# One constant in a hand-written order: the fourth Fourier sum of each batch at step 47 instead of step 48

## The chip, the cores and the metric

The kernel runs on one core of a Trainium2 chip, in float32. The metric is the device time of one execution in microseconds (us). Before the change three runs gave 2300.13, 2300.18 and 2295.85 us, so the median is 2300.13 us.

A core has five instruction streams that run side by side and wait for each other by semaphores: TensorE (PE in the profile, its weight loads PEld), VectorE (DVE), ScalarE (ACT), GpSimd (POOL) and SyncE (SP), which here only issues DMAs. Each stream runs its own instructions in the order in which they were put.

## The reference

Two blocks follow one another, for 8 batches, 12 heads, 448 positions and head width 64:

```python
scores = scale * np.matmul(q, k.transpose(0, 1, 3, 2))
scores = np.einsum('bhij,hg->bgij', scores, w_pre)
attn = softmax(scores)
attn = np.einsum('bhij,hg->bgij', attn, w_post)
x = np.matmul(attn, v)                 # then (B,H,S,D) -> (B,S,H*D)
mixed = real(fft(fft(x, axis=1), axis=2))
u = x + mixed
out = u + relu(layernorm(u) @ w_ch1) @ w_ch2
```

The first block is attention whose heads are mixed by a 12x12 matrix before and after the softmax. The second adds a two-dimensional Fourier transform of the attention's output to it, and then a feed-forward layer of width 3072.

## The kernel before, in words

**Two phases.** `mix_phase` computes u for all batches and writes it to DRAM in two tensors per batch, `u_scr` and `u_rev`. `ffn_phase` does the feed-forward layer and fills the rest of the time. In the profile the mixing phase ends at about 797 us.

**Steps.** The mixing phase is one loop over steps `s`. A batch has 23 steps, so batch b starts at step f = 23b. Each step s carries, for different rows, a softmax pipeline: "pre" (L656, mixes heads on PE from the gathered scores `Kr` into PSUM tiles `mx`), "max" (L663, DVE), "exp" (L670, ACT, into `PP`), "scale" (reciprocal on DVE at L677 and L678, then two multiplications on POOL at L680), "post" (L690, mixes heads again on PE into the PSUM tile `po`) and "turn" (L703, DVE, transposes `po` into `Pv`). "pre", "max", "exp" and "scale" of step s work for step s+2, "post" and "turn" for step s itself. "gather" (L645) issues four DMAs on SP that reorder the copied scores `Sb` into `Kr` for step s+5; `Sb` has two buffers, each for a block of three steps (one block has two), and a buffer is free when the gathers of its block have landed.

**What is put between.** Four lists hold further work with the step at which it is due. "QK" is a run of scores (L628 on PE, two PSUM tiles, copied to `Sb` by ACT at L489). "AV" is attention times v (L720, two PSUM tiles, copied to `XT` by ACT). "full" holds the transposes of q and k (L601), the turn of a finished group of rows into a tile `X` (L764, copied by ACT), `emit_z` (the first Fourier transform, L829), and `emit_s2`, the second: eight matmuls at L845 into one PSUM tile, after which DVE adds the result into two `X` tiles by four instructions (L856 and L858). A batch has four of these sums, two pairs of rows by two parities; their steps are `AT_S`. After the second parity of a pair a store goes to a list `later`, and in the "scale" part of the first step that begins with the store in that list, it is issued: an indirect DMA to `u_rev` by POOL (L868) and a DMA `u<-X` to `u_scr` on SP (L877). For pair 1 a further single row goes out on POOL (L874) two steps after that. "none" holds loads; those of v (`vv`, L581) are issued by POOL at steps 48 to 52 counted from the batch two before. `folds` are sums and differences of `X` tiles on POOL (L785, L790, L799) that `emit_z` reads later; two are issued per step after the scaling.

**PSUM.** Scores, attention times v, transposes and Fourier sums share one ring of four PSUM tiles named `ms`. A run of scores or of attention times v takes two of them, a Fourier sum one. PE waits when the tile whose turn it is has not been copied out or added yet. The copies of what is pending are put by `flush`.

**The order in a step.** On PE, DVE, ACT and POOL the order of the program is kept. It differs between even and odd steps:

```python
ORDERS = ("pre post flush AV max0 exp0 QK max1 exp1 turn scale conv full gather",
          "pre post flush max0 max1 QK exp0 AV turn exp1 scale conv gather full flush")
```

(The strings are joined here; the first is for even steps.) "conv" is one DVE operation of the preparation of the feed-forward weights (L250 to L310). On SP the order is chosen by the scheduler, which plans with its own estimates. In even steps what "full" leaves pending is flushed after the next step's "post".

**Around the change.** Steps are counted here from the start f of the batch whose sums are meant, so "step 47" is f+47. At step 46 there are a run of scores, the third Fourier sum and a turn into `X`; at step 47 a run of scores and one of attention times v; at step 48 two runs of scores and the fourth Fourier sum; at step 49 and at step 50 one run of each again; at steps 51 and 52 a run of scores and a turn into `X`. For even batches step 47 is odd and step 48 even; for odd batches the other way round. Batch 7 is not concerned, since its sums are done in the feed-forward phase in the order of the list. In batch 6 steps 47 and 48 lie behind the last softmax step, and step 47 also holds `lead.turn`, a transposition for the feed-forward phase.

Of the kernel before, what the change touches and what calls it, by code (L numbers as in the profile page):

```python
# [95 lines left out]
AT_AV = ((1, 2, 4), (0, 1, 3), (1, 3, 5), (1, 3, 4))  # L96
AT_X = ((13, 0), (23, 1), (28, 3), (29, 2))
AT_Z = (39, 40, 40, 42)
AT_S = ((42, 44), (46, 48))

ORDERS = tuple(o.split() for o in (
    "pre post flush AV max0 exp0 "
# [348 lines left out]
def mix_phase(ctx, tc, rest, ident, q, k, v, w_pre, w_post, u_scr, u_rev, wts, lead):  # L451
# [433 lines left out]
    def due(kind, at, fn):  # L885
        fill[kind].append((at, len(fill[kind]), fn))
# [4 lines left out]
    for b in range(B):  # L891
# [41 lines left out]
        for pair in range(2):  # L933
            for par in range(2):
                due("full", f + AT_S[pair][par],
                    lambda b=b, pair=pair, par=par: emit_s2(b, pair, par))
# [617 lines left out]
```

## Time and profile before

| what | value |
| --- | --- |
| median of three runs | 2300.13 us (2295.85 to 2300.18) |
| the profiled execution's own time | 2299.42 us |
| its span, first to last instruction | 2297.6 us |
| mean granted TensorE clock | 0.998 |
| busy: PE, PEld, DVE, ACT, POOL | 98%, 76%, 74%, 51%, 56% of the span |
| matmuls of the Fourier sums at L845 | 256, median 326 ns |
| adds of the Fourier sums at L856 and L858 | 64 and 64, 0.55 us each |

How to read it: the busy share of PE counts modelled ends of pipelined matmuls, so the length of a step is read from the starts of its instructions in the timeline. The list of waits says in total what an engine waited for, how often, and the longest single wait. In a timeline, brackets name the idle time ahead of an instruction and what ended it. The chain of work goes back from the last instruction of a window to what released it. In slices of 57.4 us the mixing phase takes about the first 14 of 40.

### The profile page before, as it was taken

The numbers are of one execution on the slowest core, as the hardware profiler recorded it, in microseconds if no ns is written. First come the engines' busy times: TensorE is split into PE (matmuls) and PEld (weight loads), VectorE is DVE, ScalarE is ACT, GpSimd is POOL, SyncE is SP. The second block draws the span as 40 slices with busy tenths as digits, with TensorE's granted clock in tenths as the row PEclk, the third lists the DMA queues.
The fourth block names the chain that finished last, engine by engine and source line by source line (L and its number), as shares of the span: only waits on it lengthen the run. The fifth ranks groups of instructions, "written<-read, shape, count | busy, mean of one in ns | idle before, by whom it ended". The sixth has DMA issues, their size and how long they took to land.

```text
span 2297.6 us, 60793 instructions
## 1 busy us (share of the span) xinstructions
PE 2249.2 (98%) x22894; PEld 1740.7 (76%) x22894; DVE 1711.2 (74%) x3640; ACT 1167.1 (51%) x3330; POOL 1292.1 (56%) x1805
## 2 busy tenths in 40 slices
PE   7999999999999999999999999999999999999998
PEld 3455555555554677777899999999999899999998
DVE  5778787888877757776877787778778777765545
ACT  4676767767676533231445445444444445434434
POOL 7677878879768541221555555546555645454334
PEclk9999999999999999999999999999999999999999
DMA  7566565666756475649677887788787987795664
GB/s 185 168 178 181 168 192 171 190 179 181 202 151 190 143 265 182 230 162 327 191 181 180 252 214 184 212 195 242 204 197 184 277 188 174 191 257 121 143 146 76
DMA packets 228063, 439.45 MB, mean 191 GB/s; under 512 B 35964, under 2 KB 149558, under 8 KB 227772
## 3 DMA queue, kind: packets, MB, share of 16 engines
q1 hardware_dynamic: 156620, 301.52, 38.2%
q0 software_dynamic: 68864, 133.00, 30.4%
q8 instruction: 183, 3.00, 0.6%
q10 hardware_dynamic: 2288, 1.05, 0.2%
q14 instruction: 108, 0.88, 0.1%
HBM read 213.16 MB, written 143.16 MB: 155 GB/s over the span
## 4 chain that ended last, share of the span: by engine, by line
PE 87%; DVE 5%; DMA 3%; ACT 2%; issue 1%; POOL 1%; SPq 1%; ACTq 0%; DVEq 0%; POOLq 0%
PE psP L1213 18%; PE psP L1335 14%; PE psR L1213 9%; PE psR L1335 7%; PE mx L656 6%; PE ms L720 6%; PE ms L628 5%; PE po L690 5%; PE psQ L1213 4%; PE psQ L1335 3%; PE psP L1290 3%; PE ms L845 2%; PE ms L601 2%; DMA Kr<-Sb 1%; PE psR L1290 1%
## 5 line engine op out<-in xcount | busy, mean ns | idle before, releaser
L1369 POOL DMA_DIRECT2D out_dram<-od x172 | 209.1, 1276 | 261.7 <-DVE od L1357 175.3
L680 POOL TENSOR_SCALAR PP<-PP,rcp 128x448 f32<-128x448 f32 x368 | 234.6, 647 | 170.2 <-DVE rcp L678 123.8
L670 ACT ACTIVATE PP<-mx,nmx 128x448 f32<-128x448 f32 x368 | 230.2, 631 | 165.2 <-DVE nmx L663 157.2
L663 DVE TENSOR_REDUCE nmx<-mx 128x1 f32<-128x448 f32 x368 | 212.5, 618 | 101.2 <-PE mx L656 99.1
L1176 POOL TENSOR_TENSOR hq<-h 128x128 f32<-128x128 f32 (+1 forms) x210 | 130.0, 619 | 255.9 <-ACT h L1235 122.3
L1363 ACT COPY od<-psP 128x192 f32<-128x192 f32 x488 | 156.1, 320 | 172.0 <-PE psP L1335 170.6
L1366 DVE TENSOR_TENSOR od<-od 128x768 f32<-128x768 f32 x210 | 201.3, 972 | 52.7 <-ACT od L1363 52.3
L703 DVE STREAM_TRANSPOSE Pv<-po 128x896 f32<-128x896 f32 x184 | 203.7, 1107 | 2.9 <-PE po L690 2.1
L489 ACT COPY Sb<-ms 124x448 f32<-124x448 f32 (+1 forms) x378 | 181.7, 540 | 46.0 <-PE ms L628 19.2
L656 PE MATMUL mx<-Kr,kw 60*32 60x448 f32 x2944 | 192.2, 549 | 4.3 <-ACT PP L670 2.3
L628 PE MATMUL ms<-kT,qT 64*32 64x448 f32 (+1 forms) x3072 | 191.6, 545 | 3.9 <-ACT qT L489 2.8
L720 PEld LDWEIGHTS ms<-Pv,vv 64*64 64x64 f32 x5376 | 138.1, 132 | 73.7 <-issue 48.8
L690 PE MATMUL po<-PP,kw 60*32 60x448 f32 x2944 | 184.0, 537 | 1.2 <-POOL PP L680 1.1
L1213 PE MATMUL psP<-qs,w1t 128*128 128x256 f32 x744 | 179.2, 380 | 2.4 <-DVE h L1234 1.5
L1213 PE MATMUL psP<-ks,w1t 128*128 128x256 f32 x744 | 179.3, 380 | 0.4 <-DVE h L1234 0.3
L720 PE MATMUL ms<-Pv,vv 64*64 64x120 f32 (+1 forms) x5376 | 160.8, 263 | 3.6 <-ACT Sb L489 2.2
L254 POOL TENSOR_SCALAR wst<-wst 128x256 f32<-128x256 f32 (+1 forms) x76 | 118.6, 1569 | 67.2 <-ACT wst L265 66.9
L1213 PEld LDWEIGHTS psP<-qs,w1t 128*128 128x128 f32 x744 | 139.5, 190 | 19.4 <-DVE h L1234 1.9
L1213 PEld LDWEIGHTS psP<-ks,w1t 128*128 128x128 f32 x744 | 139.5, 190 | 17.2 <-DVE h L1234 0.7
L1213 PE MATMUL psP<-ub,w1t 128*128 128x256 f32 x528 | 127.2, 379 | 1.1 <-DVE h L1234 1.1
L1234 DVE TENSOR_TENSOR h<-h,psP 128x512 f32<-128x512 f32 x42 | 28.8, 686 | 127.9 <-PE psP L1213 112.3
L1335 PE MATMUL psP<-w2t,hq 128*128 128x192 f32 x490 | 122.5, 332 | 1.2 <-DVE od L1357 1.2
(199 smaller groups left out, 5301.6 us busy)
## 6 DMA issues: line engine op xcount, KB each, us to landing
Kr<-Sb SPq DMA_DIRECT2D x730, 105.0 KB
out_dram<-od POOLq DMA_DIRECT2D x172, 384.0 KB, 6.3
qs<-ub SPq DMA_DIRECT2D x89, 384.0 KB
ks<-ub SPq DMA_DIRECT2D x88, 384.0 KB
ub<-ub SPq DMA_DIRECT2D x79, 384.0 KB
w1t<-w SPq DMA_DIRECT2D x42, 384.0 KB
w2t<-w SPq DMA_DIRECT2D x42, 384.0 KB
raw<-in_moe_w_ch_dram SPq DMA_DIRECT2D x32, 384.0 KB
```

The source lines that it names most:

```text
L628: nc.tensor.matmul(pss[x][o:o + hi - lo, :S], st["qT", xx][64 * x:64 * x + 64, y, lo:hi], st["kT", xx][64 * x:64 * x + 64, y, :], start=Tr ...
L656: nc.tensor.matmul(mx[x][64 * z + o:64 * z + o + 32, :S], kw1[64 * x:64 * x + KR, o:o + 32], Kr[64 * x:64 * x + KR, z, :], start=True, sto ...
L663: nc.vector.tensor_reduce(nmx[:, :], steps[T]["mx"][x][:, :S], axis=AX.X, op=ALU.max, negate=True)
L670: nc.scalar.activation(steps[T]["PP"][:, x, :], steps[T]["mx"][x][:, :S], ACTF.Exp, bias=steps[T]["nmx", x][:, :], accum_out=steps[T]["den ...
L680: nc.gpsimd.tensor_scalar(PP[:, x, :], PP[:, x, :], rcp[:, x:x + 1], 1.0, op0=ALU.mult, op1=ALU.mult)
L690: nc.tensor.matmul(po[o:o + 32, z, :S], kw2[64 * z:64 * z + KR, y, :], PP[64 * z:64 * z + KR, :, c * HS:(c + 1) * HS], start=True, stop=True)
L703: nc.vector.transpose(turned[a]["Pv"][:, j, :].rearrange("p (z s) -> p z s", z=2), steps[T]["po"][:, :, :S])
L720: nc.tensor.matmul(pss[y][64 * x:64 * x + 64, :nu * R], st["v", pr][64 * y:64 * y + 64, x, jb * D:(jb + 1) * D], _ap(Pv, 64 * y * rp + 32 ...
L1213: mm = nc.tensor.matmul(p[:, m, :], w1[i][:, kc, m * P:(m + 1) * P], ub[:, kc, :], start=i in (0, 4, 1)[:3 - seed] and m == kc == 0, stop= ...
L1335: nc.tensor.matmul(ps[j, key][:, :DQ], a, b, start=m in (0, 4), stop=True, skip_group_check=True)
L1366: eng.tensor_tensor(D[j][:, :, :], D[j][:, :, :], D[k][:, :, :], op=ALU.add)
L1369: nc.gpsimd.dma_start(out=acc[t, r, d], in_=D[j][:, :, :], accum_op=ALU.add)
```

## The change

The due step of the second parity of pair 1 goes from f+48 to f+47. With it move, in the program, the eight matmuls on PE, the four DVE adds behind them, and the store: the indirect DMA on POOL, the DMA on SP and the single row on POOL. For even batches the adds are flushed at the end of step 47 instead of behind "post" of step 49, so the store comes in step 48 instead of step 50. For odd batches the adds are flushed behind "post" of step 48 instead of at the end of step 48, and the store stays in step 49.

```diff
 AT_X = ((13, 0), (23, 1), (28, 3), (29, 2))
 AT_Z = (39, 40, 40, 42)
-AT_S = ((42, 44), (46, 48))
+AT_S = ((42, 44), (46, 47))
```

The numbers are used in one place:

```python
for pair in range(2):
    for par in range(2):
        due("full", f + AT_S[pair][par],
            lambda b=b, pair=pair, par=par: emit_s2(b, pair, par))
```

## The prediction

> **What bounds the kernel now.** First the head of the page: PE is busy for 98% of the span, so a wait that the change takes off PE, or puts on it, is time gained or lost.
>
> ```profile
> span 2297.6 us, 60793 instructions
> PE 2249.2 (98%) x22894; PEld 1740.7 (76%) x22894; DVE 1711.2 (74%) x3640; ACT 1167.1 (51%) x3330; POOL 1292.1 (56%) x1805
> ```
>
> Second, the list of PE's waits in the mixing phase (46 to 797 us): total, times, longest.
>
> ```profile
> PE ms L845 <- ACT Sb L489: 2.7, 6, 0.6
> ...
> PE po L690 <- POOL PP L680: 1.1, 4, 0.4
> ```
>
> The first line is what the change can remove: once in each of batches 0 to 5 the fourth Fourier sum stands behind two runs of scores until ACT has copied a tile of the ring, 0.32 us in batches 0, 2, 4 and 0.63, 0.58, 0.53 in 1, 3, 5. The second says that POOL's scaling is sometimes just late.
>
> Third, the timelines of PE at steps 47 and 48 of batch 0 (a step begins with L656), of DVE behind them, and of POOL at steps 49 to 51.
>
> ```profile
> 223.71 0.98 PE L656 MATMUL mx<-Kr,kw 60*32 60x448 f32 x16
> ...
> 227.88 0.98 PE L656 MATMUL mx<-Kr,kw 60*32 60x448 f32 x16
> ...
> 231.44 1.56 PE L845 MATMUL ms<-tcs,z 96*113 96x193 f32 x8 [0.32 <-ACT Sb L489]
> 232.93 0.98 PE L656 MATMUL mx<-Kr,kw 60*32 60x448 f32 x16
> ```
>
> ```profile
> 233.04 0.56 DVE L856 TENSOR_TENSOR X<-X,ms 113x385 f32<-113x385 f32 x1 [1.29 <-PE ms L845]
> ...
> 234.91 1.15 DVE L663 TENSOR_REDUCE nmx<-mx 128x1 f32<-128x448 f32 x2
> ```
>
> ```profile
> 237.61 1.26 POOL L680 TENSOR_SCALAR PP<-PP,rcp 128x448 f32<-128x448 f32 x2 [1.84 <-DVE rcp L678]
> ...
> 243.46 1.04 POOL L868 DMA_INDIRECT v<-X,rows  x1 [0.19 <-issue]
> ...
> 248.66 1.31 POOL L680 TENSOR_SCALAR PP<-PP,rcp 128x448 f32<-128x448 f32 x2
> ```
>
> Step 47 takes 4.17 us on PE with no wait, step 48 takes 5.05: the sum is 1.49 of it, the wait 0.32. The adds begin 1.60 us after the sum's first matmul and hold DVE for 1.87 us ahead of the next step's max. From 237.61 to 249.97 POOL never idles, and "post" of step 53 (250.02) has waited 0.24 us for it. The chain of waits that ends in that "post" runs DVE adds, max, POOL: it does not pass PE between 233 and 250.
>
> **The change part by part.**
>
> *The matmuls, even batches.* In step 47 the sum starts right behind attention times v, at 227.88 in batch 0; its ring tile was copied at about 227.45, so it waits for nothing and the 0.32 us go. The adds run 229.48 to 231.35. Step 48 is now short on PE (pre, post, two runs: 3.2 us), and DVE has the 1.87 us of adds ahead of its max. The new wait is there: "pre" of step 49 needs the two `mx` tiles that exp of step 48 reads. Before, the second exp ended 1.95 us after the adds (236.86 against 234.91); so the second half of "pre" can start at 231.35 + 1.99 = 233.34, takes 0.39, and from the start of "post" to the next step it is 3.28 us as before (233.71 to 236.99). Step 50 starts at 237.01, before at 236.99. The gain is spent inside two steps: +0.02, and likewise +0.03 in batches 2 and 4 (adds' end 423.55 and 613.78, plus 5.66, against 429.18 and 619.41). The ring doesn't bind: the second run of step 48 needs the adds' tile at 231.7, free at 231.35.
>
> *The matmuls, odd batches.* In step 47 (even) the sum stands behind a run of scores, at 323.99 in batch 1; its tile is copied by about 323.65. Adds to 327.46, then 1.99 + 0.39 + 3.31: step 50 (absolute 73) starts at 333.15, before 333.41: -0.26. Batch 3: adds to 518.69, 524.38 against 524.59: -0.21. Batch 5: 709.48, 715.17 against 715.32: -0.15. Together -0.6: of 1.74 us of waits a third is kept.
>
> *POOL, even batches.* Scaling of step 48 follows the adds by 2.70 us (234.91 to 237.61), so it moves from 231.62 to 234.05, +2.43 us, while POOL idles. Behind it now stands the indirect DMA (1.04 and 0.18 of issue), two steps earlier. Then come the folds and `vv`, which ended at 235.76, now at 239.4: scaling of step 49 is late by 1.8 us. Until the scaling of step 51, the indirect DMA's 1.22 is gone and the single row (0.56) has come: 1.8 - 1.22 + 0.56 = +1.14. So "post" of step 53 starts at 251.16, not 250.02: +1.14. Batch 2: same shift; that scaling ended 441.64, now 442.78, "post" stood at 441.76: +1.05. Batch 4: 631.19 becomes 632.34, "post" stands at 632.48: 0. Afterwards the single row is missing from the queue and the next "post" has slack. Sum +2.2. These are alternatives to the +0.02s, not added to them.
>
> *POOL, odd batches.* The store keeps its step. Scaling of step 48 comes 2.2 us later (330.15, 521.39), idle time takes most of it, 0.4 us remain in batches 1 and 3, under slacks of 0.6 at the later "post"s: 0. In batch 5 1.2 us remain; the two "post"s at 723.87 and 727.76, which wait for POOL, slip, but attention times v at 730.27 waits 1.52 us for a landing of `Kr`, which covers it: 0.
>
> *SP, even batches.* `u<-X` moves past two steps of gathers. Where the scheduler puts it is not in the trace. Batch 1 has the same distance, a step from adds to store, and there 16 gather DMAs stand between its two `u<-X` (315.50 and 332.40); the last four start at 329.10, right after the copies of block 3 ended at 329.08, so they are the gather of step 49, which the program puts behind the store: a store whose adds are fresh goes one gather later. By that row, the nearest, `u<-X` of an even batch goes behind the gather of step 48 (batch 0: issued by 229.84) and ahead of the next, which waits for copies until 235.1 anyway: 0. Other end: rival one.
>
> *DVE against POOL.* Where POOL doesn't idle, DVE's weight operation (one a step) meets it more often. In batch 1 L293 took 1.94 us from 336.85, beside two L785 of POOL from 336.48; its median is 0.43. Ends: nothing, and 1.5 us per even batch, 4.5. I take 0: DVE idles over 1 us ahead of most max operations. The Trainium skill, "SBUF — State Buffer", section "Who interferes with whom", has a rule that speaks against this cover: a DVE instruction with two SBUF inputs and a GpSimd instruction that reads SBUF exclude each other for the whole instruction. By it each such meeting costs up to one POOL instruction, and three of them would bring the sum to about +5; by the row's cover it stays as it is.
>
> *Batch 6.* The sum moves ahead of `lead.turn`, into step 185, and takes the ring tile that attention times v of step 187 needs second: free when the adds end, 791.35 + 1.60 + 1.87 = 794.8. That block of 1.66 us then ends at 796.5, the next at 798.15, and before it ended at 797.35: +0.8. Ends: 0 if a later landing absorbs it, and 1.49 if the sum's whole length shows.
>
> Sum: 2.2 - 0.6 + 0.8 = +2.4. The profiled execution took 2299.42 us (span 2297.6 and 1.8 around it), 0.7 below the median of 2300.13. 2299.4 + 2.4 = **2301.8 us**, 0.1% up: about no change.
>
> **The rivals.**
>
> *One, slower: the store bars the gather.* If SP keeps the program's order, `u<-X` waits for the adds (231.35), and the gather of step 48 follows from 232.0, its last DMA at 234.4 instead of about 229. Landings in the chain took 3.44 to 5.55 us (batches 3 and 1): 237.9 to 240.0. ACT's copy of scores in step 49 needs them to free `Sb`, nominally at 236.5; both copies are done 0.95 later, and attention times v of step 50, which began at 238.66, waits 0.15 to 2.25 us. Three batches: 0.4 to 6.7. The POOL loss is covered where this is larger, so the whole is +2.4 to +6.5, up to 2305.9. It passes 4.6 us (0.2%) from a landing of about 4.9 us. For it: program order is kept in batch 0's own stores; against it: batch 1.
>
> *Two, faster: the waits go and nothing takes their place.* -2.7 + 0.8 = -1.9: 2297.5. For it: every wait named above does go. Against: DVE's adds then stand ahead of a short step, and POOL's chain.
>
> *Three, slower: DVE and POOL block each other* for the 4.5 us above: 2306.
>
> *Four, either sign: the scheduler's plan shifts elsewhere.* SP, and ACT in parts of the feed-forward phase, are put by its estimates. The chain has two single landings at 1084.14 (6.02 us) and 1090.23 (5.19): 11 us are the bound both ways, 2288 to 2311.
>
> *Five: nothing is moved* is excluded, for the step number decides the place on four engines.
>
> **How the numbers follow.** 0.2%, 4.6 us, is about what a measurement of this kernel can tell from no change (its three runs span 4.3). Forecast: 0.45, of which 0.08 end slower by over 0.2% since its zeros are ends of ranges, and 0.01 faster. Rival one 0.17 (0.11 slower), two 0.10 (0.03 faster), three 0.08 (0.05 slower), four 0.20 (0.11 slower, 0.09 faster). So slower 0.35, faster 0.13, same 0.52. The forecast's own range is 2299 to 2305. The range of 8 in 10 leaves out the outer half of rival four and some of run-to-run spread: 2294.5 to 2309.
>
> **What would show it.** Right: no wait of L845 on ACT in steps 47, step 48 of batch 0 near 4.0 us up to the second half of "pre", step 50 starting within 0.1 us of now relative to step 47; POOL without idle from 234 to 251, and a wait of "post" of step 53 near 1.4 us; `u<-X` between two gathers, after the adds. Wrong: a wait of the copies of `Sb` on `Kr` in even batches (rival one), L293 or L297 of 1 us and more at steps 49 and 50 (three), or a difference that arises behind 797 us (four).

## The result, and the profile after

| | before | changed |
| --- | --- | --- |
| median | 2297.53 us (2293.83 to 2301.48, 13 runs, the three above among them) | 2303.07 us (2301.63 to 2315.58, 13 runs) |
| ratio, 95% interval | 1 | 1.0031 (1.0021 to 1.0042) |
| profiled execution, its span | 2299.42 us, 2297.6 us | 2303.09 us, 2301.1 us |

The changed kernel is slower by 0.31%, some 7 us by the ratio and 5.5 between the medians: two to three times the forecast of +2.4, and by the interval of the ratio outside the 0.2% that counted as no change.

The head of the page after shows the same work on every engine, and PE as busy as before:

```profile
span 2301.1 us, 60789 instructions
PE 2251.8 (98%) x22894; PEld 1740.1 (76%) x22894; DVE 1714.4 (75%) x3640; ACT 1169.2 (51%) x3330; POOL 1292.7 (56%) x1805
```

PE's waits in the mixing phase (46 to 797 us; total, times, longest):

```profile
PE ms L601 <- ACT Sb L489: 9.3, 20, 1.6
PE po L690 <- POOL PP L680: 2.5, 5, 1.2
...
PE mx L656 <- ACT PP L670: 1.9, 6, 0.8
```

and the same two of them before, which rose:

```profile
PE ms L601 <- ACT Sb L489: 6.9, 19, 1.2
...
PE mx L656 <- ACT PP L670: 0.8, 1, 0.8
```

The six waits of L845 on the ring, 2.7 us, are gone, as the change means to. In their place "post" waits 1.4 us more for POOL, the transposes L601 wait 2.4 us more, and "pre" waits six times for exp where before it did so once. These waits don't add up to the loss, so the steps have to be measured. PE's timeline after, steps 47 to 51 of batch 0:

```profile
220.42 0.98 PE L656 MATMUL mx<-Kr,kw 60*32 60x448 f32 x16
...
224.85 1.56 PE L845 MATMUL ms<-tcs,z 96*113 96x193 f32 x8
226.34 0.98 PE L656 MATMUL mx<-Kr,kw 60*32 60x448 f32 x16
...
229.81 1.20 PE L656 MATMUL mx<-Kr,kw 60*32 60x448 f32 x12 [0.22 <-ACT PP L670]
230.63 0.60 PE L690 MATMUL po<-PP,kw 60*32 60x448 f32 x4
230.82 0.56 PE L656 MATMUL mx<-Kr,kw 60*32 60x448 f32 x4
...
232.81 1.71 PE L720 MATMUL ms<-Pv,vv 64*64 64x120 f32 x56
234.45 0.98 PE L656 MATMUL mx<-Kr,kw 60*32 60x448 f32 x16
...
242.63 0.98 PE L601 MATMUL ms<-ident,rawq 128*128 128x128 f32 x7 [0.77 <-ACT Sb L489]
```

The sum (224.85) waits for nothing now. "Pre" of step 49 (229.81) is in pieces, 12 matmuls and 4, with the first of "post" between them, and the transposes of step 51 wait 0.77 us. Before, they waited 0.23:

```profile
244.63 0.98 PE L601 MATMUL ms<-ident,rawq 128*128 128x128 f32 x7 [0.23 <-ACT Sb L489]
```

DVE and ACT behind the sum, after the change:

```profile
226.45 0.56 DVE L856 TENSOR_TENSOR X<-X,ms 113x385 f32<-113x385 f32 x1 [1.90 <-PE ms L845]
...
228.31 1.15 DVE L663 TENSOR_REDUCE nmx<-mx 128x1 f32<-128x448 f32 x2
...
237.92 2.26 DVE L250 TENSOR_SCALAR tmp<-raw 128x256 uint32<-128x256 uint32 x1
240.11 0.61 DVE L663 TENSOR_REDUCE nmx<-mx 128x1 f32<-128x448 f32 x1
```

```profile
229.03 0.63 ACT L670 ACTIVATE PP<-mx,nmx 128x448 f32<-128x448 f32 x1 [3.40 <-DVE nmx L663]
...
230.26 1.83 ACT L489 COPY Sb<-ms 124x448 f32<-124x448 f32 x4
```

Exp of step 48 starts 2.69 us after its step (229.03 - 226.34), and before it started 1.74 us after it (229.62 - 227.88). The four copies of scores behind it end at 232.09. The last two lines of DVE are a weight operation in step 50 and the max of step 51. Before, the weight operation was short and DVE then idled until the max:

```profile
240.46 0.49 DVE L250 TENSOR_SCALAR tmp<-raw 128x256 uint32<-128x256 uint32 x1
...
242.10 1.16 DVE L663 TENSOR_REDUCE nmx<-mx 128x1 f32<-128x448 f32 x2 [1.13 <-PE mx L656]
```

POOL and SP after the change:

```profile
231.01 1.27 POOL L680 TENSOR_SCALAR PP<-PP,rcp 128x448 f32<-128x448 f32 x2 [2.63 <-DVE rcp L678]
232.45 1.04 POOL L868 DMA_INDIRECT v<-X,rows  x1 [0.17 <-issue]
...
237.84 1.97 POOL L785 TENSOR_TENSOR xs<-X 113x384 f32<-113x384 f32 x2
...
246.89 1.32 POOL L680 TENSOR_SCALAR PP<-PP,rcp 128x448 f32<-128x448 f32 x2
```

```profile
228.43 0.32 SPq L877 DMA_DIRECT2D u<-X  x1
232.12 14.97 SPq L645 DMA_DIRECT2D Kr<-Sb  x17
```

`u<-X` goes out right behind the adds (they end at 228.31), and SP is then idle until the copies of scores are done.

**Where the time lies.** The step lengths on PE, from start to start of "pre", after less before, in us, in these two profiled executions:

| batch | steps 47 to 49 | 50, 51 | 52 to 54 | sum |
| --- | --- | --- | --- | --- |
| 0 | +0.75 | +0.54 | +0.23 | +1.52 |
| 1 | +0.20 | +0.24 | +0.81 | +1.25 |
| 2 | +0.46 | +0.66 | +0.39 | +1.51 |
| 3 | +0.38 | +0.41 | 0.00 | +0.79 |
| 4 | +0.50 | +1.07 | 0.00 | +1.57 |
| 5 | +0.46 | +0.11 | +1.18 | +1.75 |
| all | +2.75 | +3.03 | +2.61 | +8.39 |

Outside these steps the batches differ by -1.4 us in sum, in single steps that differ by 0.2 to 1.3 us either way, such as the one before with 1.1 us of "issue" ahead of a third sum (L845), which is not there after. From the first sum of batch 0 to that of batch 6 this makes +6.99 (570.47 to 577.46 us). But the changed execution came to that first sum 1.98 us sooner (202.39 instead of 204.37), ahead of anything that the change moves. The end of batch 6 gives 0.5 back, so the feed-forward phase starts 4.5 us later, and at the end of this pair of executions +3.5 is left. I rely on the ratio for the whole, and on the table for its parts.

### The profile page after: what moved, and what is told of

The parts are those of the page before. It is cut to its first block, busy times and chain, and to the rows that moved or that the text cites. A ratio compares the mean times of both kernels' runs of the same rounds, so it can differ in the third digit from the quotient of the medians.

```text
span 2301.1 us, 60789 instructions
## 1 busy us (share of the span) xinstructions
PE 2251.8 (98%) x22894; PEld 1740.1 (76%) x22894; DVE 1714.4 (75%) x3640; ACT 1169.2 (51%) x3330; POOL 1292.7 (56%) x1805
## 3 DMA queue, kind: packets, MB, share of 16 engines
q10 hardware_dynamic: 2288, 1.05, 0.2%
## 4 chain that ended last, share of the span: by engine, by line
PE 81%; DVE 5%; issue 4%; POOL 4%; DMA 3%; ACT 2%; SPq 1%; DVEq 0%; ACTq 0%; POOLq 0%
PE psP L1213 17%; PE psP L1335 14%; PE psR L1213 8%; PE psR L1335 7%; PE mx L656 6%; PE ms L720 5%; PE ms L628 5%; PE psQ L1213 4%; PE po L690 4%; PE psQ L1335 3%; DMA Kr<-Sb 2%; PE ms L845 2%; PE psP L1290 2%; PE ms L601 1%; PE ms L829 1%
## 5 line engine op out<-in xcount | busy, mean ns | idle before, releaser
L656 PE MATMUL mx<-Kr,kw 60*32 60x448 f32 x2944 | 200.3, 551 | 6.8 <-DMA Kr<-Sb 3.4
```

The lines of the kernel that those rows point to most:

```text
L656: nc.tensor.matmul(mx[x][64 * z + o:64 * z + o + 32, :S], kw1[64 * x:64 * x + KR, o:o + 32], Kr[64 * x:64 * x + KR, z, :], start=True, sto ...
```

## The experiments

Theory A: the four adds now stand ahead of the short step 48, so exp of step 48 is late, "pre" of step 49 is split, and the loss is in steps 48 and 49. Theory B (the forecast's main term): POOL's queue, through the indirect DMA that comes two steps sooner in even batches. Theory C (rival three): DVE's weight operations meet POOL's multiply. Theory D (rival one): `u<-X` on SP holds the gather. All ratios are against runs of the kernel before on the same chip, with 95% intervals; "growth" is the table's sum, 8.39 us for the changed kernel, from one profiled execution each.

**One parity at a time.**

```diff
-                due("full", f + AT_S[pair][par],
+                due("full", f + AT_S[pair][par] + (pair == par == 1 and b % 2 == 1),
```

(and with `b % 2 == 0` for the odd batches alone)

> Only the even batches (0, 2, 4, 6) have their fourth sum a step sooner; the odd ones keep it in step 48. [...] If each batch pays its own loss (the split 'pre', 0.47, in every batch; meetings of DVE and POOL), this kernel is +3 to +4.5 us to before. If the loss is POOL's, whose indirect DMA moves in even batches alone (my forecast's main term), the whole of it, +5 to +7, is here. If it comes of SP's gather, moved past the store in every batch, about half, +3 to +4.

Measured: 1.0023 (1.0012 to 1.0033), +5.3 us; growth 5.01.

> Only the odd batches (1, 3, 5) have their fourth sum a step sooner. My forecast put -0.6 on these three batches (the wait of L845 goes and nothing comes): by it this kernel is 0.6 us faster than before. By the split 'pre' (+0.47 per batch) and the meetings of DVE and POOL it is +2.5 to +4 us slower. By POOL's queue alone it is even with before, within 0.5.

Measured: 1.0012 (1.0003 to 1.0021), +2.8 us; growth 4.81, of which 3.29 in batch 5 alone. The two add up to 8.1 us, near the whole of 7 (4.8 to 9.7 by its interval). Odd batches lose where I forecast a gain: steps 47 to 49 grow by 0.20, 0.39 and 0.44 us in batches 1, 3 and 5. So POOL's early indirect DMA, which odd batches don't have, isn't the whole cause. The even batches' +5.3 lies in the range of "POOL alone", with an interval (2.8 to 7.6) that holds "each batch its own loss" too. Some 1.3 us of the even batches' growth are not in the changed kernel: step 49 takes 5.08 to 5.09 us there (4.65 in the changed kernel), with attention times v interrupted (0.43 us between two of its starts in batch 0, 235.30 to 235.73). Why is open.

**The stores at their old steps in even batches.**

```diff
-            later.append(store)
+            if pair and b % 2 == 0 and b < B - 2:
+                later.append(lambda: later.append(lambda: later.append(store)))
+            else:
+                later.append(store)
```

> The sum a step sooner in every batch, but in batches 0, 2 and 4 the second pair's stores are issued where before issues them, in step 50: the indirect DMA of POOL, u<-X and the single row stand at their old places. By POOL's queue (my forecast: +1.14 and +1.05 in batches 0 and 2) and by the store's place on SP, the wait of 'post' in step 53 of batch 0 is back at about 0.24 us, the gather follows the scores of step 48 sooner, and the kernel is 2 to 3 us faster than the changed one. By the adds (split 'pre' in step 49) and by the meetings of DVE's weight operation with POOL's multiply, neither of which this touches, it is within 0.5 us of the changed kernel, and the 6.14 us from the adds' end to step 50 stay.

Measured: 1.0024 (1.0014 to 1.0035), 1.6 us less than the changed kernel, which the intervals don't separate from nothing (between the medians it is 1.8 us more). POOL's indirect DMA is back at its place, but "post" of step 53 in batch 0 still waits 0.43 us, so that wait is not the indirect DMA's alone. The 0.47 us of step 49 stay too: steps 48 and 49 take 8.10 us as in the changed kernel. SP's order is not the one I expected: it keeps `u<-X` right behind the adds, with 12 gather DMAs between the two stores of a batch as in the changed kernel (16 before). One thing did go: the long step 51. It takes 4.45 us in batches 0 and 2 (4.98 and 5.11 in the changed kernel, 4.44 and 4.45 before). So the early store does cost in even batches, by another way than I had it; more on that below.

**Without the adds.**

```diff
-            for back in range(2):
+            for back in range(2 if (pair, par) != (1, 1) or b > 5 else 0):
```

> The changed kernel with DVE's four adds of the fourth sum left out in batches 0 to 5 (the output lacks that part); matmuls, copies and stores stay. If the adds ahead of the short step 48 make the exp late, split 'pre' in step 49 and hold SP's gather behind the late scores, all of that goes: L656 in step 49 isn't split, adds' place to step 50 falls by 0.47 per batch and more, POOL's scaling comes about 1.5 us sooner, and the kernel is 5 to 12 us faster than the changed one (the adds' own DVE time, 1.87 us in six batches, goes too: 11.2 is the bound). If POOL's indirect DMA or the store's place on SP is the cause, the wait of 'post' in step 53 (L690 on POOL) stays at about 0.5 us in batch 0 and the kernel is less than 3 us faster.

Measured: 1.0014 (1.0004 to 1.0024), 3.9 us less than the changed kernel; growth 1.73 instead of 8.39. The output of this kernel lacks that part of the sum. The change in time is below the 5 us that theory A asked for and above the 3 that the others allowed; the profile decides. Steps 48 and 49 of batch 0, PE:

```profile
228.57 0.98 PE L656 MATMUL mx<-Kr,kw 60*32 60x448 f32 x16
...
231.60 1.06 PE L656 MATMUL mx<-Kr,kw 60*32 60x448 f32 x16
232.36 1.05 PE L690 MATMUL po<-PP,kw 60*32 60x448 f32 x16
```

Step 48 takes 3.03 us (3.47 with the adds) and "pre" of step 49 is in one piece. Over the six batches together steps 47 to 49 are 0.57 us shorter than before, where with the adds they are 2.75 longer. That is -0.49 to -0.74 in each odd batch, but +0.11 to +0.61 in the even ones: in their step 49 (4.64 to 4.70 us) attention times v is interrupted here too, as with the even batches alone (in batch 2 it took 2.21 us from 425.02, against 1.71 in the changed kernel). So the even batches don't decide here, and the next kernel has to. Step 53 of batch 0 stays at 4.74 us (4.76 in the changed kernel, 4.52 before), so about 0.2 us there don't come of the adds.

**The adds earlier.** Leaving out work also takes away its time. So the next kernel keeps the adds and moves the sum inside step 47: ahead of attention times v in odd steps, ahead of the scores in even ones, in batches 0 to 5.

```diff
 ORDERS = tuple(o.split() for o in (
     "pre post flush AV max0 exp0 "
-    "QK max1 exp1 turn scale conv full gather",
-    "pre post flush max0 max1 QK exp0 "
-    "AV turn exp1 scale conv gather full flush"))
+    "max1 exp1 turn scale conv sum QK full gather",
+    "pre post flush max0 max1 QK exp0 exp1 "
+    "sum AV turn scale conv gather full flush"))
...
-                due("full", f + AT_S[pair][par],
+                due("sum" if pair == par == 1 and b < B - 2 else "full", f + AT_S[pair][par],
```

(Without "sum" in them the new strings leave the order of instructions on every engine as it was.)

> The sum stays in step 47 but stands ahead of attention times v in odd batches and ahead of the scores in even ones, so that DVE's four adds start 1.5 to 1.7 us earlier and are done before the max of step 48 is ready. If the adds ahead of the short step 48 are the cause, exp of step 48 no longer waits 3.4 us for its max, L656 of step 49 isn't split, the scores' copies and with them SP's gather come earlier, and of the 8.4 us that steps 47 to 54 of the six batches grew, about 6 go, as where the adds were left out (8.4 to 1.7): 5 to 7 us faster than the changed kernel, near the kernel before (-1 to +1.5). If POOL's queue or the place of u<-X on SP is the cause, or the meetings of weight operations with POOL, it stays within 1.5 us of the changed kernel.

Measured: 1.0002 (0.9990 to 1.0013), 6.7 us less than the changed kernel; growth 2.35. This is theory A's number. DVE and PE of batch 0:

```profile
228.65 0.55 DVE L858 TENSOR_TENSOR X<-X,ms 113x383 f32<-113x383 f32 x1
229.86 1.16 DVE L663 TENSOR_REDUCE nmx<-mx 128x1 f32<-128x448 f32 x2 [0.67 <-PE mx L656]
```

```profile
225.65 1.56 PE L845 MATMUL ms<-tcs,z 96*113 96x193 f32 x8
...
228.84 0.98 PE L656 MATMUL mx<-Kr,kw 60*32 60x448 f32 x16
...
231.87 1.06 PE L656 MATMUL mx<-Kr,kw 60*32 60x448 f32 x16
...
234.36 1.71 PE L720 MATMUL ms<-Pv,vv 64*64 64x120 f32 x56
```

Max of step 48 now waits for PE and not PE's next "pre" for max. Steps 48 and 49 together take 7.15 to 7.17 us in even batches and 7.35 to 7.43 in odd ones; in the changed kernel they take 8.10 to 8.14. That is 0.95 and 0.75 us a batch, about 5 us in six, of the 6.7, in even batches as in odd ones. Step 51 stays long (5.00 and 5.12 us in batches 0 and 2), so its loss has another cause.

**No weight operation in steps 49 and 50,** in the changed kernel and in the one before:

```diff
-                    if s >= 4:
+                    if s >= 4 and (s < 46 or s % GS not in (3, 4)):
```

> The changed kernel with no weight operation of DVE in steps 49 and 50 of any batch (they are done in other steps). If their meetings with POOL's multiply (L250 and L293 took 2.26 and 2.18 us beside L785) make the wait of L601 in step 51, that wait falls from 0.77, 0.70, 0.90 and 1.01 us (batches 0 to 3) to the 0.23 to 0.6 us of before, and the kernel is 1.5 to 2 us faster than the changed one. If the late exp of step 48 makes it, through the copies of the scores that ACT does behind it, the wait stays within 0.2 us of the changed kernel's and so does the time, within 0.5 us.

> The kernel before with no weight operation of DVE in steps 49 and 50. It tells what this by itself is worth: by the meetings (rival three), nothing is to be had here, since in the kernel before the waits of L601 in step 51 were 0.23 to 0.60 us; 0 to -0.5 us. A gain as large as in the changed kernel would say that the meetings are not what the change brought.

Measured in the changed kernel: 1.0035 (1.0022 to 1.0048), no gain; in the kernel before: 0.9991 (0.9980 to 1.0002). The step that it was aimed at behaves as theory C says. In batches 0 to 3 step 51 takes 4.45, 4.47, 4.45 and 4.48 us, where the changed kernel takes 4.98, 4.94, 5.11 and 5.25. The kernel before gains there too, but less: 4.48 and 4.47 us in batches 1 and 3 instead of 4.70 and 4.85, and nothing in batches 0 and 2. So odd batches had such meetings already, and the change made them longer and brought those of even batches. Changed kernel without the weight operations, batch 0, DVE at step 51 and the transposes:

```profile
242.95 1.16 DVE L663 TENSOR_REDUCE nmx<-mx 128x1 f32<-128x448 f32 x2 [1.54 <-PE mx L656]
```

```profile
245.48 0.98 PE L601 MATMUL ms<-ident,rawq 128*128 128x128 f32 x7 [0.23 <-ACT Sb L489]
```

Max starts 1.01 us after its step (241.94) and not 1.55 (240.11 - 238.56). But the time was wrong by 2 us and more. The postponed weight work moves other things: "post" of step 53 of batch 0 waits for nothing, with the weights' two DMAs (L243, L234) gone from the part of POOL's queue ahead of it. And in step 53 of batch 4 both kernels lose much more, 5.4 us (9.39) in the changed one and 7.3 (11.38) in the one before. ACT there, without the weight operations in the kernel before:

```profile
636.94 0.97 ACT L489 COPY Sb<-ms 124x448 f32<-124x448 f32 x2 [5.87 <-DMA Kr<-Sb]
```

A landing of the gather is late. Why just there, and whether the postponed work has to do with it, was not settled.

**Early sum and late stores.** Both edits, the sum early in step 47 and the stores of batches 0, 2 and 4 in step 50:

> The sum early in step 47 as in the kernel before this one in the list, and in batches 0, 2 and 4 the stores in step 50 as before. By POOL's queue the wait of 'post' in step 53 of batches 0 and 2 (0.24 and 0.4 us more than before) goes too: 0.5 to 1.5 us faster than with the early sum alone. By the adds as the whole cause it is even with it, within 0.5.

Measured: 0.9995 (0.9985 to 1.0006), 1.6 us less than with the early sum alone, with overlapping intervals. Step 53 doesn't get shorter, against the expectation (4.89 and 4.38 us in batches 0 and 2, 4.74 and 4.44 with the early sum alone). What goes is step 51 again: 4.45 us in both batches, 5.00 and 5.12 with the early sum alone. Batches 0 to 4 together are 0.4 us shorter than before; batch 5 is 3.08 longer, 1.43 of it in step 53, behind a landing.

**Batch 5 left at step 48,** and then also no weight operation in step 50:

```diff
-                due("sum" if pair == par == 1 and b < B - 2 else "full", f + AT_S[pair][par],
+                due("sum" if pair == par == 1 and b < 5 else "full",
+                    f + AT_S[pair][par] + (pair == par == 1 and b == 5),
...
-                    if s >= 4:
+                    if s >= 4 and (s < 46 or s % GS != 4):
```

(the second hunk only in the second kernel)

> The sum early in step 47 and the stores of batches 0, 2 and 4 in step 50, as in the last of the earlier list, but batch 5 keeps its fourth sum in step 48. There steps 47 to 54 of batches 0 to 4 were 0.15 longer, 0.46 shorter, even, 0.11 and 0.01 shorter than before, and batch 5 was 3.08 us longer, at the wait of the copy of Sb for Kr in step 53. By the late scores as the cause of that wait, step 53 of batch 5 is back near 6.7 us, and with the end of batch 6 (0.5 sooner in the changed kernel) the sum is -1 us against before: even, or just faster. If that wait comes and goes by itself (it was 6.1 to 8.8 us over the kernels), step 53 of batch 5 is as likely to stay near 8 us and the kernel is 1 to 2 us slower than before.

Measured: 1.0005 (0.9993 to 1.0017): even with before. Step 53 of batch 5 takes 5.93 us; over all these kernels it took 5.8 to 8.8, with no order that I could find, so this run doesn't tell a cause from chance.

> The kernel before this one in the list, and no weight operation of DVE in step 50 alone, where it met POOL's multiply L785. Without weight operations in steps 49 and 50 the wait of L601 in step 51 was 0.23 us in batches 0 to 3, and 'post' of step 53 in batch 0 waited nothing (4.04 us instead of 4.76), with the indirect DMA of POOL still early: so by the meetings step 51 is at 4.46 us in every batch, step 53 of batch 0 at about 4.05, and the kernel is 1.5 to 2.5 us faster than the one before this in the list, and 2 to 3.5 faster than the kernel before. If the delay of POOL comes from its indirect DMA, step 53 of batch 0 stays at 4.5 or more. A landing of Kr in step 53 of batch 4 that took 5 us longer where two steps went without weight operations can come again and cost that.

Measured: 0.9990 (0.9982 to 0.9999), 2.3 us faster than before: the only version whose interval lies below 1, and only just; among so many versions one such interval can be chance. The transposes of step 51, batch 0:

```profile
244.55 0.98 PE L601 MATMUL ms<-ident,rawq 128*128 128x128 f32 x7 [0.23 <-ACT Sb L489]
```

Step 51 takes 4.45 to 4.48 us in all of batches 0 to 4, so the weight operation of step 50 alone was the one that cost. Step 53 of batch 0 takes 4.18 us, near the 4.05 expected, with 4.84 in the kernel without this edit; but in batches 1 and 2 it takes 5.02 and 4.86. The late landing came here in step 53 of batch 3 (8.79 us instead of 4.07), so the profiled execution isn't faster than that before; the median is.

## Why the prediction was right or wrong

The time of 2303.07 us lies in the forecast's own range of 2299 to 2305, but the sum was too small: forecast +2.4, measured +5.5 between the medians and +7 by the ratio. "Same", which I held likeliest with 0.52, did not come. That the range held is partly luck. Its base of 2299.4 lies 1.9 us above the median of 13 runs; with the measured +7 it would have given 2306. And the sum came near for other reasons than its own: its largest term, +2.2 for POOL in even batches, measured about 0.6, while most of the loss came from two places that the sum left out: 2.9 us by which the late second half of "pre" was mis-sized, and 1.85 for DVE's meetings with POOL, put at 0.

Of the signs named in advance three came: no wait of L845, no idle time on POOL, `u<-X` between two gathers. Three did not: from step 48 to the second half of "pre" it took 4.48 us (226.34 to 230.82) and not 4.0, step 50 starts 0.75 us later after step 47 and not within 0.1, and "post" of step 53 waits 0.48 us and not 1.4. The sign of rival three came: at steps 49 and 50 L297 took 1.10 us in batch 0 and L293 2.18 in batch 1 (1.94 before).

- **Right: the waits of L845 go**, adds start 1.60 us after the sum's first matmul (226.45 - 224.85) and hold DVE for 1.86, and POOL's scaling follows them by 2.70 (231.01 - 228.31).
- **Wrong size, the main one: the second half of "pre" "can start at 231.35 + 1.99 = 233.34, takes 0.39", and then 3.28 us to the next step.** From the adds' end to step 50 I had 5.66 us; it is 6.14 in batch 0 (228.31 to 234.45) and 6.15 in batch 1 (324.77 to 330.92). The second exp ends at 230.28, 1.97 us after the adds, as I had it. But the last piece of "pre" starts at 230.82 and not at 230.30, behind twelve matmuls that began at 229.81 and four of "post"; from there to step 50 it is 3.63 us, about the 3.67 that I had. The whole block is slower on PE: "pre", "post" and the run of scores of step 49 took 3.00 us (229.81 to 232.81), and in one piece 2.49 (231.87 to 234.36, with the early sum). The starts of single matmuls in the trace show where it goes: undisturbed they come eight at a time, some 0.38 us apart (232.93, 233.33 and 233.71 in the kernel before), in the split block four at a time (229.81, 230.21, 230.42, 230.63), so the half whose operands are there runs without the other. I had priced the split at the speed of undisturbed steps. It is 0.48 a batch, 2.9 us in six. With it the odd batches' -0.26, -0.21 and -0.15 become +0.2 to +0.3; measured in steps 47 to 49 are +0.20, +0.38 and +0.46. That the adds' place does it is shown by moving them (steps 48 and 49 lose 0.75 to 0.95 us in every batch) and, in odd batches, by taking them away.
- **Wrong: "DVE against POOL: I take 0".** The price was in the bounds (up to 1.5 us per even batch) and rival three had it, but the cover, DVE's idle time ahead of max, was misread. It is over 1 us in 44 of the 179 steps of the mixing phase before, not in most (the line below). At step 51 of batch 0 it was 1.13 us, and L250 took 1.77 us longer beside L785 (2.26 instead of 0.49): max came 0.54 later, and through exp and the copies the transposes waited. In batch 1 L293 held it for 2.18 us beside L785 (1.97), in batch 2 L310 for 2.38 (0.65 before). Steps 51 of batches 0 to 3 grew by 1.85 us together, all of it gone without the weight operations. The rule in the Trainium skill, "SBUF — State Buffer", section "Who interferes with whom", that I set aside is what these rows look like: L293 has two SBUF inputs, and the page names `tensor_scalar`, which L250 is, among those that can contend for the shared port pair, under conditions that no run here tests. In these rows DVE was held over two POOL instructions one after the other, ending 0.3 to 0.5 us after the second. DVE's waits ahead of max in the kernel before (46 to 797 us; total, times, longest):

```profile
DVE nmx L663 <- PE mx L656: 94.0, 109, 1.7
```

- **POOL, even batches: the largest term, +2.2, and wrong.** "Post" of step 53 in batch 0 comes 1.53 us later after step 47's start (27.84 instead of 26.31), where I had 1.14, but only 0.24 of it is a longer wait for POOL; PE itself was late by then. Steps 53 of batches 0 and 2 grew by 0.23 and 0.39 us, and not even that is shown to be the indirect DMA's: with the stores at their old steps "post" in batch 0 still waits 0.43 us. What the early indirect DMA did cost was elsewhere: its 1.04 us stand ahead of L785 on POOL and push it into the weight operation. With the stores late, step 51 of batches 0 and 2 is back at 4.45 us. In batch 4, where I had 0, step 50 grew by 1.55, where "pre" stopped for 1.05 us from start to start (622.08 to 623.13, 0.51 of it listed as "issue"), and step 51 shrank by 0.48; other kernels have such stops at other places, and I don't count it for the change.
- **SP: placed wrongly, harmless.** `u<-X` is not behind the gather of step 48 but ahead of it. Rival one is out all the same: SP idles from 228.75 to 232.12 and the gather starts when the copies end, 232.09. In batches 2 and 4 the gather starts as closely behind the copies (426.23 after 426.21, 619.34 after 619.31). What holds the gather is the late copies, not the store.
- **Odd batches, landings: "attention times v waits 1.52 us for a landing of `Kr`, which covers it".** It didn't: the landing itself came later (wait 1.70), behind a "post" in step 52 that waited 1.24 us for POOL; it is +1.18 in batch 5, 1.00 of it in step 52. Batch 1 lost 0.81 to a copy that waited 1.64 us for a landing. These come and go over the kernels (batch 1's step 53 took 4.06 to 5.25 us), so how much belongs to the change stays open.
- **Batch 6: +0.8 became -0.5.** From its first sum to the feed-forward phase 21.95 us, before 22.48. The wait for the adds' ring tile, which made the +0.8, is not there: attention times v runs on in one go (798.23, 3.65 us for 112 matmuls).

So the sum with the terms as measured: -0.5 + 2.9 + 0.3 (a longer run of scores in step 47 of batch 0) for the matmuls, +1.85 for step 51, +0.6 for step 53 in batches 0 and 2, up to +2 in batches 1 and 5, where landings come in, -0.5 at the end: about +5 to +7.

## What to carry to other kernels

When work moves out of one step into another, ask what stands ahead of the *shorter* step on every other engine: here PE's wait of 0.3 to 0.6 us went, and 1.9 us of DVE work was left alone ahead of a step that PE finishes in 3 us. A late operand that came in halves cost more than its lateness here, because the block that it split ran slower; price it from a row that shows a split, or give it a range. If the adds can be put a microsecond or two earlier, into idle time, the same move costs nothing that could be measured here (1.0002). A shift of POOL's queue should be checked for which DVE operation it will now stand beside.

## What the hardware showed that I had not expected

- A block of 48 matmuls (60x448, "pre", "post", scores) in which operands came in two portions took 3.00 us on PE from its first start, and 2.49 us when they came at once: half a microsecond that no list of waits has, since the only wait listed (0.22 us) lies ahead of the block.
- A DVE operation that took 0.49 us at its place before (L250, 128x256) took 2.26 us when it began 0.08 us behind POOL's pair of L785 (1.97 us), and 1.09 us when it began 1.27 us behind the pair (stores late, 241.74): in both it ended about 0.4 us after POOL's second instruction.
- One step (53) took 4.0 to 11.4 us in batch 4 and 5.8 to 8.8 us in batch 5 over kernels that differ little, the long ones behind a landing of one gather (5.87 us of wait in the longest). A single profiled execution can be 5 us off for that alone, as much as the whole change.
